# The opening of a fused attention and feed-forward kernel, laid out anew by hand

## The chip, the cores and the metric

The kernel runs on one core of a Trainium2 chip, alone. The metric is the device time of one execution in microseconds; lower is better. The median of three runs before the change is 768.19 us (765.53 to 770.01).

The core's engines are named as in the profile: PE multiplies matrices (PEld loads its weights), DVE and POOL work elementwise, ACT evaluates functions and casts, SP issues DMA transfers. Each works through its own list of instructions in order and waits on semaphores for the others.

## The reference

```python
x = A_x                                             # 2048 x 512
mod = (_silu(c) @ w_mod).reshape(c.shape[0], 6, 1, -1)
sa, ca, ga, sb, cb, gb = (mod[:, 0], ..., mod[:, 5])     # six vectors of 512
h = _layernorm(x, axis=-1) * (1 + ca) + sa
x = x + ga * _A_ref(h, A_wq, A_wk, A_wv, A_wo, A_beta)   # 32 heads of 16, 4 segments of 512 rows, causal softmax plus a memory of earlier segments
h = _layernorm(x, axis=-1) * (1 + cb) + sb
x = x + gb * _B_ref(h, B_w1, B_b1, B_w2, B_b2)           # squared relu, 512 -> 1792 -> 512
```

All is float32. The change concerns what happens before the first attention products: the vectors `ca` and `sa` (numbers 1 and 0 of the six), the normalized first 512 rows, and the weights Wq, Wk, Wv.

## The kernel before

The kernel writes its work as nodes (`op(engine, ...)`), each with an engine, the nodes that it needs and the buffers that it takes. `Plan.run` puts them in order. For each engine a table `ORDER` gives node numbers, and the node at the table's front is taken as soon as its needs are met; behind the table's end the planner goes by priorities. So the table is the order in which an engine's instructions stand in the program, and a node that waits holds up all behind it on its engine.

Numbers are kept exact by splitting: a value is cast to a high part (on ACT), and a subtraction gives the low part (on DVE or POOL); a product is then three matmuls, high by high, high by low and low by high.

The opening, in the order of what needs what:

- The vector c (512 values) is loaded, put through the silu on ACT and DVE, transposed on PE (L532, tile `bcs`) and copied to `cs`, four columns of 128.
- `ca` comes by `mod_cols` and `mod_parts` (L549 to L595): four loads of 256 KB each (`wmod`, L555), one product of four matmuls that fill the four column groups of PE (L570, `bmod`; the "four-fold product" below), a copy on ACT (L574), four matmuls of one column each that sum and turn it (L592), and a DVE instruction that puts it into `modc` (L594). The matmuls are float32 and each appears as two records in the trace.
- `sa` comes by `mod_pieces` (L598 to L614): four loads (L602), and after each of them four matmuls of 128x128 weights by one column (L608). It needs no copy.
- The first 512 rows of x are loaded in four tiles (`xt`, L662), their statistics taken on DVE (L618), the root on POOL (L623), the rows normalized (L627). PE turns them in four groups of four transposes (L640, "turns"). Each turned group is scaled and shifted by `ca` and `sa` (ACT L644 for groups 0 and 2, DVE L647 for 1 and 3), cast to the high part (ACT L650) and given its low part (DVE L651).
- Wq, Wk and Wv are loaded in two transfers each, a first block of 128 columns and the rest (L710). Each has four blocks of columns; ACT casts each (L720), POOL makes the low part (L724; DVE that of Wv's first). The raw Wq lies in `X1L`.
- For the first head group the products of Wq and Wk with all rows are 24 matmuls (L804, two sets of twelve, one for Wq and one for Wk); the later groups take half-height matmuls in groups of six (L810, each pair of sets eight groups), V also in groups of six (L880). Evictions (L841, L843) put the results into `sg`, and transfers on SP ("fills", L859) lay them out in `ST`, whose unused rows six clearing transfers zero beforehand (L736). Score products that find the row maxima (L918, `ba`) follow.
- The two halves of `w1`'s preparation that matter here: a load into `X1L` (L754), which waits until all low parts of Wq are made, and casts and stores of it (L763, L766), piece by piece.

Fillers (L542, `bwarm`) are products of the identity with itself, which nothing reads: 70 of them, placed by the table.

Of the kernel before, what the change touches and what calls it, by code (L numbers as in the profile page):

```python
# [13 lines left out]
ALU = mybir.AluOpType  # L14
# [19 lines left out]
N_WARM = 70  # L34
# [23 lines left out]
8-24 3 25-28 94 29 95-96 30-32 97 33-35 86 36-39 88 117 121 109 113 40-62 283 63-73 284 74-76 285 77 277-280 286  # L58
436-438 322 439 323-324 441 325 442-443 339 353 444 327-330 360 595-596 368 597-598 344 381 600-601 350 602 347 374
603 305-307 356 308 540 371 310-311 465 365 312 386 313 470 721 389 722 377 723 473 393 724 396 860 864 868 479 726  # L60
401 727 476 728 486 497 729 384 405 482 409 406-407 412 500 416 511 419 491 424 513 872 494 624 543 428-430 545 876
552 629 877 548 878 666 879 638 555 432 881 560 882 632 883 503 884 635 645 519 564 669 565-566 521 641 568 1045 575
659 1046 571 1047 578 1048 750 758 535 792 583 1050 764 653 537 587 795 588-589 671 985 1051 678 1052 681 1053 656
909-910 650 911-912 674 755 914-915 686 662 916 761 917 771 779 690-692 767 785 926 694 591 927 943 928 951 929 1120
701 931-932 709 933 1180-1181 957 697 934 1182 776 1183 704 713 988 782 1185 797 1186 800 1187 788 1188 964 978 991
714-715 804 948 1463 1467 954 807 816 812 972 1255 820 817-818 960 827 1315 823 975 1316 830 1317 1078 969 1318 835
1471 1475 1086 1320 1123 1321 1083 981 1322 1099 1113 1323 717 839 994 1126 840 997 1107 841 1001 1089 1004 1092 1009
1013 843 1017 1258 1014 1095 1020 1104 1024 1110 1027 1015 1261 1213 1227 1032 1224 1036-1037 1116 1129 1218 1038 1136
1221 1479 1132 1480 1139 1481 1144 1040 1482 1234 1242 1148-1150 1152 1393 1484 1159 1230 1485 1245 1167 1486 1155
1248 1162 1487 1390 1348 1396 1171-1173 1264 1529-1530 1239 1271 1531-1532 1267 1175 1279 1534-1535 1274 1362 1536  # L70
1251 1537 1356 1512 1369 1513 1377 1514 1591 1515 1359 1353 1283-1285 1287 1517 1290 1294 1518 1380 1519 1365 1520
1374 1648 1383 1649 1546 1650-1651 1297 1302 1554 1653-1655 1386 1560 1656 1551 1306-1308 1783-1784 1399 1310 1402
1785-1786 1567 1575 2070 2074 1788 1406 1588 1409 1789 1557 1790 1414 1791 1578 2066 2078 1418 1563 1581 1594
1419-1420 1572 1681 1723 1422 1918 1429 1919 1432 1920 1686 1425 1921 1695 1437 1923 1692 1441 1597 1924 1600 1925
1584 1926 1689 1702 1442-1443 1707 1604 1607 1716 1726 1616 1713 1612 1617 1620 1858 1698 1618 1729 1623 1710 1627
1630 1445 1816 1639 1635 1821 1732 1640 1861 1824 1735 1641 1739 2082 1742 1830 2083 1747 2084 1719 2085 1837 1851
1643 1751-1752 1864 1753 1755 1845 2087 1758 2088 1827 1762 2089 1765 1993 1770 2090 1848 1833 1774-1776 1842 2111
1951 1959 2112 1867 2113 1854 2114 1965 1874 1778 2116 1882 2117 1877 2118 1870 2119 1956 2240-2241 1962 2187 1972
2242-2243 1980 1968 1886-1888 1986 1890 2245 1983 2246 2145 2247 1996 2248 2150 1893 2128-2129 1897 2130-2131 1977
1900 2133 1905 2134 1989 2156 2135 2166 2136 2180 2177 527 1909-1911 2002 2159 2364 2005 2365 2009 2171 2366 2153 2367  # L80
2012 1913 2369 2017 2370 2174 2371 2162 2372 2290 2301 2021-2023 2025 2311 2032 2488-2489 2295 2028 2490 2183 2491
2040 2304 2035 2493-2494 2298 2269 2044 2277 2495 2190 2496 2193 2045-2046 2197 2274 529 2200 2048 2205 1999 2209 2280
2213 2210-2211 2307 2220 2216 2435 2223 2630 2283 2228 2232-2233 2286 2393 2234 2407 2398 2640 2633-2636 2314 2321
2643-2644 2329 2404 2317 2650 2645-2646 2324 2401 2236 2414 2653 2660 2654-2656 2663 2670 2333-2335 2337 2344 2428
2664-2666 2410 2352 2340 2517 2525 2673-2674 2347 2531 2675 2710 2676 2419 2438 2528 2356-2358 2422 2522 2713 2680
2714-2716 2445 2425 2448 2683-2684 2720 2685-2686 2431 2453 2360 2441 2538 2723 2759 2724 2751 2690 2725-2726 2461
2534 2457 2552 2468 2464 2458-2459 2476 2471 2549 2693 2763 2755 2694-2696 2730 2562 2546 2565 2480-2482 2543 2569
2733-2734 2555 2572 2484 2577 2735 2700 2736 2581 2585 2588 2592 2582-2583 2559 2595 2600 2703-2706 2740 2604-2606
2743 2608 2744-2746 2892 2894 2893 2808 2798 2895 2898 2897 2801-2802 2788 2896 2811 2803 2791 2804 2792 2818 2812
2793 2813-2814 2821-2823 2794 2916 2915 2917 2824 3055 2920 2918 3054 2919 3053 2921 3056 3058 2938 3135 2941 3057  # L90
2939 2943 2940 3059-3060 3123 2942 2944 3065 2961-2962 3063 3061 2967 2963 3071 3069 2964 3070 2965-2966 3067 2985
3073 2984 2987 3075 2986 3131 3072 3077 2990 2989 2988 3074 3078 3127 3081 3007 3076 3009 3008 3082 3012 3079-3080
3010 3013 3084 3011 3030 3088 3032 3031 3083 3036 3086 3085 3090 3033 3035 3092 3089 3087 3094 3163 3091 3095 3093
3034 3165 3098 3096 3166 3099 3167 3100 3103 3164 3104 3102 3097 3107 3190 3108 3168 3106 3115 3169 3112 3388 3101
3184-3185 3105 3186 3109 3188 3187 3189 3311 3380 3118 3205 3208 3206 3313 3310 3207 3392 3211 3317 3210 3209 3312
3226 3314 3316 3227-3228 3384 3230 3324 3229 3329 3322 3231 3318 3247 3232 3315 3248 3320 3250 3326 3249 3328 3333
3327 3252-3253 3331-3332 3337 3251 3330 3271 3335-3336 3268 3273 3270 3269 3341 3334 3340 3272 3339 3289 3292 3338
3345 3290 3274 3344 3343 3349 3291 3295 3342 3346-3347 3353 3293 3348 3294 3350 3421 3420 3649 3352 3424 3422 3357
3351 3641 3356 3354 3361 3423 3637 3355 3359 3358 3363 3426 3365 3425 3375 3360 3441 3364 3372 3442-3443 3445 3444
3362 3366 3369 3447 3446 3463 3467 3568-3569 3464 3462 3466 3567 3468 3570 3465 3571 3574 3483 3486 3485 3484 3573  # L100
3579 3575 3572 3488 3585 3581 3487 3505 3645 3577 3586 3583 3489 3587 3508 3589 3584 3504 3588 3591 3507 3506 3510
3590 3509 3595 3593 3526 3594 3597 3592 3596 3525 3527-3528 3530 3601 3600 3598 3604 3529 3547 3531 3546 3549 3608
3548 3605 3599 3602 3551 3603 3612 3550 3607 3606 3678 3552 3610 3609 3680 3611 3613 3615 3677 3614 3679 3616 3683
# [293 lines left out]
def block_kernel(ctx, tc, x, wq, wk, wv, wo, beta, w1, b1, w2, b2, c, wmod, out):  # L397
# [1238 lines left out]
```

## Time and profile before

| | |
|---|---|
| median of 3 runs | 768.19 us (765.53 to 770.01) |
| profiled execution, its own time | 769.3 us |
| its span, first to last instruction | 767.6 us |
| mean granted PE clock | 0.991 |
| PE busy | 753.6 us, 98% of the span, 6641 instructions |
| DVE, ACT, POOL busy | 585.1, 431.4, 321.5 us |

The profiled execution lies 1.1 us above the median of the runs. The page cuts the span into 40 slices of 19.2 us and prints one digit for each; a nine is 90% or more. Since a waiting matmul's end is modelled, a busy PE need not be a useful one, and fillers count as busy. The timeline gives start and length of each merged group of instructions, and in brackets the idle time of the engine before it and what ended it. The chain of waits goes back from the last instruction to what released it.

### The profile page before, as it was taken

The page shows a single profiled execution, that of the slowest core. Times are in us where ns is not written, and L with a number is a line of the kernel's source. Part 1 is how long each engine was busy: PE and PEld are TensorE (multiplying, and loading weights), DVE is VectorE, ACT ScalarE, POOL GpSimd, SP SyncE. Part 2 cuts the span into 40 slices and gives each one's busy share as a digit, 9 for nine tenths or more (in the row PEclk, how much of TensorE's full clock was granted, in tenths as well). Part 3 has the DMA queues.
Part 4 walks back from the last instruction along what each step waited for, and adds up shares of the span by engine and source line. Part 5 has one row for each costly group of instructions (what it writes and reads, how often), then busy time and mean ns, then how long its engine had stood idle before and what let it go on. Part 6 is the DMA issues. An engine that isn't in the chain of part 4 may idle for free.

```text
span 767.6 us, 17957 instructions
## 1 busy us (share of the span) xinstructions
PE 753.6 (98%) x6641; PEld 607.3 (79%) x6641; DVE 585.1 (76%) x1585; ACT 431.4 (56%) x958; POOL 321.5 (42%) x400
## 2 busy tenths in 40 slices
PE   9999999999999999999999999999999999999997
PEld 7987667765786667776666678998998898989986
DVE  4378898888899887888999986879774875576544
ACT  1558988799978986688856835455211412121110
POOL 4564876688968776366241632351020002000000
PEclk8899999999999999999999999999999999999999
DMA  9478674544665333557573055764552554448721
GB/s 307 160 208 223 202 238 119 156 131 142 173 185 139 96 86 80 172 126 196 173 232 120 3 203 175 287 229 151 192 188 106 188 192 168 151 163 274 273 96 56
DMA packets 61057, 129.65 MB, mean 169 GB/s; under 512 B 8613, under 2 KB 23977, under 8 KB 59178
## 3 DMA queue, kind: packets, MB, share of 16 engines
q1 hardware_dynamic: 60818, 128.37, 52.9%
q8 instruction: 53, 0.87, 0.5%
q14 instruction: 34, 0.28, 0.1%
q10 hardware_dynamic: 152, 0.13, 0.1%
HBM read 81.29 MB, written 20.19 MB: 132 GB/s over the span
## 4 chain that ended last, share of the span: by engine, by line
PE 86%; ACT 4%; DMA 3%; SPq 2%; POOL 2%; DVE 1%; issue 1%; ACTq 0%; POOLq 0%; DVEq 0%
PE bh L1516 18%; PE bqk L810 9%; PE bpv L1146 7%; PE bpf L1579 7%; PE bpf L1578 7%; PE bpf L1580 7%; PE bpb L1087 5%; PE bv L880 5%; PE ba L918 5%; PE bwarm L542 3%; PE bwop L1248 2%; ACT pt L1104 2%; PE bwop L1250 2%; PE bwop L1249 2%; PE bmr L1011 1%
## 5 line engine op out<-in xcount | busy, mean ns | idle before, releaser
L923 DVE CUSTOM_DVE_ANT_0 ba<-ba,msk 128x384 f32<-128x384 f32 (+2 forms) x384 | 192.9, 531 | 35.8 <-PE ba L918 25.1
L1104 ACT ACTIVATE pt<-bpb 128x512 f32<-128x512 f32 x320 | 172.2, 619 | 21.8 <-PE bpb L1087 16.6
L1091 POOL TENSOR_SCALAR_AFFINE_SELECT pt<-pt 128x512 f32<-128x512 f32 x128 | 79.6, 641 | 74.9 <-ACT pt L1104 58.8
L810 PE MATMUL bqk<-HT,WQK 64*128 64x512 f32 x720 | 105.7, 397 | 0.0
L1087 PE MATMUL bpb<-ST 64*128 64x256 f32 (+2 forms) x512 | 79.3, 348 | 2.8 <-DVE sg L843 1.3
L1146 PE MATMUL bpv<-pt,VT 128*32 128x512 f32 (+3 forms) x1024 | 80.3, 437 | 1.1 <-POOL ac L959 0.3
L918 PE MATMUL ba<-ST 63*128 63x256 f32 (+2 forms) x512 | 75.9, 342 | 3.1 <-DMA ST<-sg 1.8
L810 PEld LDWEIGHTS bqk<-HT,WQK 64*128 64x128 f32 x720 | 70.6, 185 | 9.1 <-issue 0.9
L1087 PEld LDWEIGHTS bpb<-ST 64*128 64x128 f32 x512 | 51.3, 186 | 25.1 <-ACT pt L1104 7.4
L1560 ACT CAST ST<-xx 128x512 fp32r<-128x512 f32 x43 | 26.6, 620 | 69.4 <-DVE xx L1552 55.0
L918 PEld LDWEIGHTS ba<-ST 63*128 63x128 f32 x512 | 51.0, 186 | 17.9 <-issue 6.5
L1516 PE MATMUL bh<-ST 128*128 128x256 f32 x420 | 59.1, 282 | 0.0
L1516 PEld LDWEIGHTS bh<-ST,w 128*128 128x128 f32 x420 | 56.2, 190 | 3.4
L1516 PEld LDWEIGHTS bh<-ST 128*128 128x128 f32 x420 | 56.0, 189 | 3.1
L1516 PE MATMUL bh<-ST,w 128*128 128x256 f32 x420 | 58.3, 282 | 0.0
L880 PE MATMUL bv<-WVO,HT 64*128 64x512 f32 x384 | 56.5, 404 | 0.7 <-DVE mx L923 0.7
L1146 PEld LDWEIGHTS bpv<-pt,VT 128*32 128x32 f32 x1024 | 28.7, 109 | 33.6 <-issue 24.6
L923 DVE DVE_READ_ACCUMULATOR2_ANT mx<- 128x1 f32 x384 | 54.2, 141 | 0.0
L1347 POOL TENSOR_TENSOR tt<-h2raw 128x512 f32<-128x512 f32 x8 | 11.0, 1388 | 99.1 <-ACT h2raw L1312 77.7
L1578 PE MATMUL bpf<-w,ST 128*128 128x512 f32 x132 | 52.1, 395 | 0.0
L1579 PE MATMUL bpf<-w,ST 128*128 128x512 f32 x132 | 52.0, 394 | 0.0
L1580 PE MATMUL bpf<-w,ST 128*128 128x512 f32 x132 | 51.7, 391 | 0.0
(210 smaller groups left out, 1630.7 us busy)
## 6 DMA issues: line engine op xcount, KB each, us to landing
ST<-w1d SPq DMA_DIRECT2D x14, 1792.0 KB
w<-w1d SPq DMA_DIRECT2D x14, 1792.0 KB
ST<-sg SPq DMA_DIRECT2D x192, 128.0 KB
w1d<-X1L SPq DMA_DIRECT2D x21, 512.0 KB
xt<-in_A_x SPq DMA_DIRECT2D x16, 256.0 KB
wm<-in_w_mod SPq DMA_DIRECT2D x16, 256.0 KB
xw<-in_A_x SPq DMA_DIRECT2D x16, 256.0 KB
X1L<-in_B_w SPq DMA_DIRECT2D x7, 512.0 KB
```

Source lines behind the costliest of these rows:

```text
L810: nc.tensor.matmul(bank(banks[w]), W3(w, k, x, cols.start, cols.stop)[r], HT[r, y, k], start=first and i == 0, stop=last and i == 2)
L880: nc.tensor.matmul(bank(banks[t]), HT[r, x, k, (t2 + t) * P:(t2 + t + 1) * P], WVO[r, k, y], start=first and i == 0, stop=last and i == 2)
L918: nc.tensor.matmul(dst[:, c0:c0 + n], ST[b:b + 63, 0, sl, qt * P:(qt + 1) * P], ST[b:b + 63, 1, sl, :n], start=True, stop=True)
L923: nc.vector.tensor_tensor_reduce(i, i, msk[:, 512 - n:], scale=1.0, scalar=-3e38, op0=ALU.add, op1=ALU.max, accum_out=o)
L1087: nc.tensor.matmul(dst, ST[b:b + 64, 1, sl, kb * P:(kb + 1) * P], ST[b:b + 64, 0, sl, q0:512], start=True, stop=True)
L1091: nc.gpsimd.affine_select(out=ap, in_=ap, pattern=[[0, ap.shape[1]], [1, P]], compare_op=ALU.is_ge, fill=0.0, base=0, channel_multiplier=-1)
L1104: ns = [op("ACT", 0.49, lambda j=j: nc.scalar.activation(buf("PPP"[n], pt)[:, i + j], bank(keys[j]), AF.Exp, scale=0.25), pr[slot] + 0.01 ...
L1146: nc.tensor.matmul(bank(o)[32 * hq:32 * hq + 32, q0:q0 + src.shape[1]], v[:, a:a + 32], src, start=start, stop=stop, tile_position=(0, 32 ...
L1516: nc.tensor.matmul(pb(i), A[:, x, kk], B[:, y, kk], start=kk == j == 0, stop=kk == 1 and j == 2)
L1578: nc.tensor.matmul(q, rh, wh, start=(i == 0), stop=False)
L1579: nc.tensor.matmul(q, rh, wl, start=False, stop=False)
L1580: nc.tensor.matmul(q, rl, wh, start=False, stop=(i == NF - 1))
```

## The change

Three things change, and nothing behind the opening.

1. `sa` is made as `ca` is, by `mod_cols`; `mod_pieces` is gone.
2. 40 fillers instead of 70.
3. The tables begin with another order. With the numbers shifted for the missing nodes, the lists differ for PE in its first 210 entries of some 1300, for ACT in 130 of 940, for DVE in 87 of 895, for POOL in 53 of 342, for SP in 103 of 403, and are the same behind that. (The trace shows these places before 105 us.)

```diff
-N_WARM = 70
+N_WARM = 40
...
     "PE": """
-8-24 3 25-28 94 29 95-96 30-32 97 33-35 86 36-39 88 117 121 109 113 40-62 283 63-73 284 74-76 285 77 277-280 286
...
+8-30 3 31-33 56 34-37 58 64 82 78 38 66 39-40 90 86 41-47 246-249 252-255 405-408 291 410-413 292-293 308 322 294
...
-    def mod_pieces(m, slot, plus, pr):
-        key, b = ("wmod", m), ("modc", m)
-        loads, n = [], None
-        for k in range(KD):
-            loads.append(sp(lambda k=k: nc.sync.dma_start(buf("P", key)[:, k] if not k else TL[key][:, k],
-                                                          wmod[k * P:(k + 1) * P, m * D:(m + 1) * D]),
-                            pr + 0.001 * k, 1 << 18, get=() if k else [("P", key)], soft=loads[:1]))
-
-        def mm(k):
-            for j in range(KD):
-                nc.tensor.matmul(bank(b)[:, j:j + 1], TL[key][:, k, j * P:(j + 1) * P], cs[:, k:k + 1],
-                                 start=k == j == 0, stop=k == j == KD - 1)
-        for k in range(KD):
-            n = pe("F", 1.05, lambda k=k: mm(k), pr + 0.02 + 0.001 * k, after=[n_cs, loads[k], n], get=() if k else [("#D", b)],
-                   put=[key])
-        return dve(4, lambda: nc.vector.tensor_scalar(modc[:, slot, :], bank(b)[:, 0:KD], plus, None, op0=ALU.add),
-                   pr + 0.05, after=[n], put=[b])
-
...
     n_ca = mod_cols(1, CA, 1.0, PR0 + 0.1, True)
-    n_sa = mod_pieces(0, SA, 0.0, PR0 + 0.2)
+    n_sa = mod_cols(0, SA, 0.0, PR0 + 0.2, True)
```

Lines behind L597 move up by 18: L640 becomes L622, L804 becomes L786, L724 becomes L706, L859 becomes L841.

PE, from the four-fold product of `ca` on, before (xN counts equal matmuls in a row; `bwarm` are fillers, `blnq` turns, `bqk` the first head group's products):

```order
L570 MATMUL bmod<-wmod,cs 32x512 x4
L542 MATMUL bwarm<-ident 128x128 x4
L592 MATMUL bmodc<-selc,t 128x1 x4
L640 MATMUL blnq<-ident,xt 128x128 x16
L542 MATMUL bwarm<-ident 128x128 x23
L804 MATMUL bqk<-HT,WQK 128x512 x3
L542 MATMUL bwarm<-ident 128x128 x11
L804 MATMUL bqk<-HT,WQK 128x512 x3
L542 MATMUL bwarm<-ident 128x128 x3
L804 MATMUL bqk<-HT,WQK 128x512 x3
L542 MATMUL bwarm<-ident 128x128
L804 MATMUL bqk<-HT,WQK 128x512 x15
```

Ahead of these rows stood 17, 4, 1, 3 and 3 fillers, with the transpose L532 and the sixteen matmuls of L608 between them. PE from the same place after the change:

```order
L570 MATMUL bmod<-wmod,cs 32x512 x4
L542 MATMUL bwarm<-ident 128x128 x4
L592 MATMUL bmodc<-selc,t 128x1 x4
L570 MATMUL bmod<-wmod,cs 32x512 x4
L622 MATMUL blnq<-ident,xt 128x128 x8
L542 MATMUL bwarm<-ident 128x128
L592 MATMUL bmodc<-selc,t 128x1 x4
L542 MATMUL bwarm<-ident 128x128 x2
L622 MATMUL blnq<-ident,xt 128x128 x8
L542 MATMUL bwarm<-ident 128x128 x7
L786 MATMUL bqk<-HT,WQK 128x512 x24
L792 MATMUL bqk<-HT,WQK 128x512 x24
```

Ahead of these now stand 23 fillers, the transpose, and three fillers. The 24 products stand in one piece, and those of Wq come before those of Wk (before, nine of Wk's came first). The turns are parted, and the second vector's two steps stand around their first half.

POOL's low parts of the weights, before (raw Wq is `X1L`, raw Wk and Wv are `w`; the second row's order by the table is Wq's block 3, 1, 0, 2):

```order
L624 TENSOR_TENSOR mv<-mv,nhalf 128x2
L724 TENSOR_TENSOR WQK<-w,WQK 128x4x128
L724 TENSOR_TENSOR WQK<-X1L,WQK 128x4x128 x4
L724 TENSOR_TENSOR WQK<-w,WQK 128x4x128
L724 TENSOR_TENSOR WVO<-w,WVO 128x4x128 x3
L724 TENSOR_TENSOR WQK<-w,WQK 128x4x128
```

and after, where the blocks are Wq 0, Wk 0 and 1, Wq 1, Wv 1 to 3, Wq 3, Wk 2, Wq 2:

```order
L606 TENSOR_TENSOR mv<-mv,nhalf 128x2
L706 TENSOR_TENSOR WQK<-X1L,WQK 128x4x128
L706 TENSOR_TENSOR WQK<-w,WQK 128x4x128 x2
L706 TENSOR_TENSOR WQK<-X1L,WQK 128x4x128
L706 TENSOR_TENSOR WVO<-w,WVO 128x4x128 x3
L706 TENSOR_TENSOR WQK<-X1L,WQK 128x4x128
L706 TENSOR_TENSOR WQK<-w,WQK 128x4x128
L706 TENSOR_TENSOR WQK<-X1L,WQK 128x4x128
```

Wq's first block moved from third to first place, Wq's block 2 to the last.

SP's transfers, before (from the seventh on; `ST<-pad` are the clearing transfers):

```order
L555 DMA wmod<-in_w_mod 128x512 x2
L662 DMA xt<-in_A_x 128x512
L555 DMA wmod<-in_w_mod 128x512
L710 DMA w<-in_A_wk 128x4x128
L555 DMA wmod<-in_w_mod 128x512
L710 DMA w<-in_A_wk 128x4x384
L710 DMA w<-in_A_wv 128x4x128
L710 DMA X1L<-in_A_wq 128x4x128
L710 DMA X1L<-in_A_wq 128x4x384
L736 DMA ST<-pad 32x4x512 x4
L710 DMA w<-in_A_wv 128x4x384
L736 DMA ST<-pad 32x4x512 x2
```

and after, from the sixth on (the first seven of `wmod` are the last three loads of `ca` and the four of `sa`):

```order
L555 DMA wmod<-in_w_mod 128x512 x7
L692 DMA X1L<-in_A_wq 128x4x128
L692 DMA w<-in_A_wk 128x4x128
L692 DMA w<-in_A_wk 128x4x384
L692 DMA w<-in_A_wv 128x4x128
L692 DMA X1L<-in_A_wq 128x4x384
L692 DMA w<-in_A_wv 128x4x384
L718 DMA ST<-pad 32x4x512 x2
L535 DMA ge<-in_A_beta 128x32
L718 DMA ST<-pad 32x4x512 x2
L644 DMA xt<-in_A_x 128x512 x2
L841 DMA ST<-sg 32x2x512 x6
```

The loads of `ca` moved ahead of those of `sa`, Wq's first block ahead of the other weights. The third pair of clearing transfers went down among the fills, behind the first store of w1; the w1 load, which stood ahead of the next rows of x and of all fills, now stands behind the first seven fills, and two of the four loads of the next rows of x stand among the fills.

More of the change, by code (lines that the diff above doesn't have):

```diff
@@ L190 @@
+3850
 """,
     "POOL": """
[L192 to L195 removed]
@@ L206 @@
+2320 2312 2319 2718 2413 2420-2421 2510 2425 2444 2443 2448 2436 2735-2737 2537 2738 2545 2544 2549 1970 2560 2568
+2567 2572 2798 2802 3347 2807 2811 2843 3090 2816 2825 2820 2829 2834 2847 2852 2856 3107 3109 2838 3108 3110 3604
+3364 3366 3365 3367 3621-3622 3624 3623
 """,
     "SP": """
[L208 to L209 removed]
```

296 lines of the change are left out of this document (146 added, 150 removed), and 14 rows, old and new, of the table ORDER.

## The prediction

> **What bounds the kernel now.** I read the page's head and slices first, then a table by stretch, then the opening in order of time, then the chain of waits and the DMA issues of SP. Head: busy share of PE, and granted clock by slice.
>
> ```profile
> PE 753.6 (98%) x6641; PEld 607.3 (79%) x6641; DVE 585.1 (76%) x1585; ACT 431.4 (56%) x958; POOL 321.5 (42%) x400
> PEclk8899999999999999999999999999999999999999
> ```
>
> PE is busy for 98% of the span, so only PE time that does nothing, or PE time at a low clock, can be won. The table by stretch says where such time is (columns: stretch, length, busy us and instructions of PE, PEld, DVE, ACT, POOL, granted clock, DMA share, GB/s).
>
> ```profile
> 9.90:13.30 3.40, 3.40 (x33) 3.40 (x32) 1.15 (x3) 0.00 (x0) 0.93 (x2) 1.00 1.07 367
> 14.00:21.00 7.00, 7.00 (x33) 5.11 (x33) 0.66 (x4) 1.10 (x2) 1.26 (x1) 0.50 1.10 344
> 25.00:34.00 9.00, 9.00 (x75) 8.64 (x74) 4.19 (x5) 6.89 (x14) 5.75 (x5) 1.00 0.02 7
> 60.00:70.00 10.00, 9.34 (x87) 7.93 (x83) 8.93 (x30) 7.26 (x23) 2.92 (x5) 1.00 0.76 214
> 70.00:80.00 10.00, 8.44 (x99) 5.97 (x99) 6.90 (x23) 9.19 (x19) 4.94 (x6) 1.00 0.82 229
> ```
>
> The clock is 0.50 from 14 to 21 us, and PE counts as busy throughout the first three rows. What it is busy with, the timeline shows (start, us, engine, line, operation, count):
>
> ```profile
> 1.90 6.22 PE L542 MATMUL bwarm<-ident 128*128 128x128 f32 x34 [1.90 <-POOL ident masks.py:199]
> 10.01 0.47 PE L542 MATMUL bwarm<-ident 128*128 128x128 f32 x2
> 12.02 0.91 PE L542 MATMUL bwarm<-ident 128*128 128x128 f32 x6
> 15.42 1.94 PE L570 MATMUL bmod<-wmod,cs 128*32 128x512 f32 x8
> 17.50 0.58 ACT L574 COPY t<-bmod 128x512 f32<-128x512 f32 x1 [9.03 <-PE bmod L570]
> 19.16 1.71 PE L592 MATMUL bmodc<-selc,t 128*128 128x1 f32 x8
> 20.73 3.30 PE L640 MATMUL blnq<-ident,xt 128*128 128x128 f32 x16
> 20.90 0.16 DVE L594 TENSOR_SCALAR modc<-bmodc 128x4 f32<-128x4 f32 x1 [6.34 <-PE bmodc L592]
> 23.86 5.30 PE L542 MATMUL bwarm<-ident 128*128 128x128 f32 x46
> 29.69 2.62 PE L542 MATMUL bwarm<-ident 128*128 128x128 f32 x22
> ```
>
> L542 is a filler (each is two records). From 23.86 to 32.3 PE runs 34 fillers and three useful products (L804). The useful work proper, which from here on leaves PE almost no pause, begins later, in the chain of waits:
>
> ```profile
> 34.61 3.45 PE bqk L804 x15
> 44.53 1.39 PE bqk L810 x12
> 45.92 0.55 PE ba L918 x8
> 70.90 1.46 PE blnq L640 x12
> 83.01 0.99 PE bmod L570 x8
> 85.23 0.98 PE bmodc L592 x8
> ```
>
> What keeps the useful work back is in POOL and DVE: the low parts of the weights (L724) and of the normalized rows (L651, inputs from L647).
>
> ```profile
> 18.68 1.26 POOL L724 TENSOR_TENSOR WQK<-w,WQK 128x512 fp32r<-128x512 f32 x1 [5.69 <-ACT WQK L720]
> 22.71 0.81 DVE L647 TENSOR_SCALAR lnf<-blnq,modc 128x512 f32<-128x512 f32 x1 [1.65 <-PE blnq L640]
> 26.07 2.50 DVE L651 TENSOR_TENSOR HT<-lnf,HT 128x512 fp32r<-128x512 f32 x4 [1.20 <-ACT HT L650]
> 28.20 5.66 POOL L724 TENSOR_TENSOR WQK<-X1L,WQK 128x512 fp32r<-128x512 f32 x4 [8.26 <-ACT WQK L720]
> 35.07 3.79 POOL L724 TENSOR_TENSOR WVO<-w,WVO 128x512 fp32r<-128x512 f32 x3
> ```
>
> POOL waited 8.26 us for a cast and only then made the four low parts of Wq, to 33.86. The first block of Wq stands third of the four, so the second half of the first head group's products could not start before about 32.5. So the bound of the opening is: modulation vectors at 21.06, low parts of the rows to 28.57, low parts of Wq, while PE fills.
>
> **The change, part by part.** Durations at full clock are from the chain above: a four-fold product 0.99, its four column products 0.98, four turns 1.46/3 = 0.49; a filler record 5.30/46 = 0.115, so a filler 0.23.
>
> *Up to the second vector.* 23 fillers stand first, 46 records: the first 34 took until 8.12, twelve more make 9.50; the transpose of the silu (0.22) and three fillers, 10.41. The first vector's four loads are now fourth to eighth in the queue. Landing: the tenth load of before is the one waited for here.
>
> ```profile
> 10.98 0.69 DVE L618 BATCH_NORM_STATS2 bs<-xt 128x6 f32<-128x512 f32 x1 [1.41 <-DMA xt<-in_A_x]
> ```
>
> At 344 to 367 GB/s (the first two rows by stretch) a load of 256 KB takes some 0.75 us, so the eighth has landed by 9.5 and the twelfth by 12.5. The product of the first vector runs 10.4 to 11.4, its copy (0.14 after it, 0.58) to 12.1 under four fillers (to 12.3), its columns to 13.3; the second vector's product, all loads there, to 14.3; its copy to 15.0 lies under eight turns (to 15.3) and a filler (15.5); columns to 16.5, and the vector (0.16 on DVE) stands at 16.7, against 21.06. The 32 one-column records (L608, two for each product of the order's rows) go, 16 records come. Of the 4.4 us won some 1.7 are clock: at half clock the product and the columns cost 1.94 and 1.71 instead of 0.99 and 0.98 (and the sixteen turns behind them 3.30 instead of 1.96).
>
> Does the clock stay full? In before it halves and returns here (columns: PE busy, clock, DMA):
>
> ```profile
> 13.20:13.40 0.20, 0.20 (x3) 0.20 (x3) 0.20 (x1) 0.00 (x0) 0.00 (x0) 0.70 1.05 369
> 23.40:23.60 0.20, 0.20 (x3) 0.20 (x2) 0.12 (x1) 0.05 (x1) 0.00 (x0) 0.70 1.08 407
> 78.20:81.60 3.40, 2.10 (x30) 1.09 (x28) 2.05 (x6) 2.61 (x7) 0.85 (x2) 1.00 0.21 75
> 296.60:300.00 3.40, 2.53 (x20) 1.44 (x13) 2.65 (x7) 3.24 (x8) 0.00 (x0) 1.00 0.02 5
> 300.00:303.40 3.40, 3.40 (x20) 3.35 (x19) 2.96 (x12) 1.93 (x5) 2.00 (x2) 0.50 0.19 39
> ```
>
> 23.5 less 13.3 is 10.2, and the second dip lasts 3.4, so the clock seems to be judged in steps of 3.4 us. The step to 13.3 held only 4 fillers, 0.9 us; the rest was one-column products. The step to 300 was busy for 2.53 and lost the clock, the one from 78.2 was busy for 2.10 and kept it; since the ends of matmuls are modelled, I count both by records and the spacing of their kind in the chain (0.23 or 0.117) and get about 1.8 for either. So the border lies near 1.8 of 3.4. After the change any 3.4 us between 10 and 17 hold at least 2.25 us of fillers, four-fold products and turns (12.3 to 15.7 is the thinnest): I take the clock as full, and hold half clock as a rival. The Trainium skill, "TensorE: Matmul & The Clock Gate", Part 1: The HAM clock gate, has the clock halve after an idle window of about 3.4 us; by it neither kernel would dip, and this trace disagrees: the row 9.9 to 13.3 shows PE busy for 3.40 of 3.40. The Trainium skill, the same page, Part 4: PE-mode transpose, says that transposes do not count as work for the clock. By that rule the thinnest 3.4 us here would hold 1.25 us, the clock would halve, and the time would be the rival's, 763. The trace speaks against it: the clock returns at 23.5 after a step that held almost only turns.
>
> *Up to the first products.* DVE makes two of the shifted rows (0.81 each, the second after turns that end at 17.4) to 18.4 and the first low part (2.50/4 = 0.63; 0.7 with its start) to 19.1. PE: two fillers, eight turns, seven fillers, 16.5 + 0.46 + 0.98 + 1.61 = 19.5. ACT, at 0.6 a cast and 0.8 a shifted row as in the rows above, has cast the four high parts by about 20.9, so the third low part comes at 21.1 and PE waits 0.3. Wq's and Wk's first low parts are no longer behind anything: their loads are 13th and 14th, casts after 15.0, POOL 15.6 to 18.4 with two of 1.3 to 1.4. All 24 records of L804 then run in one piece: 24 x 0.23 = 5.5, plus waits, to 25.4. Before they ended at 38.06: 12.7 earlier. The 38 fillers among and ahead of them become ten.
>
> *Up to the first score product.* Wk's and Wq's second low parts: casts behind the rows' casts, at 22.2; POOL to 25.0. Then four groups of the second head group (0.70 each) to 28.2; POOL's three parts of Wv (3.79 in all) to 28.9, which costs PE some 0.9; one V group, four and two more groups, 7 x 0.70, to 34.0. That is eleven groups, as many as before had done at 45.92. Gain 12. SP gives the same:
>
> ```profile
> 38.79 5.89 SPq L859 DMA_DIRECT2D ST<-sg  x9
> 16.79 3.81 SPq L736 DMA_DIRECT2D ST<-pad  x2
> 47.37 0.57 SPq L766 DMA_DIRECT2D w1d<-X1L  x1
> 51.14 3.29 SPq L859 DMA_DIRECT2D ST<-sg  x5
> ```
>
> The fills of ST (L859, 0.65 each) wait for the last eviction of the first head group, 25.4 + 0.6 + 0.7: from 26.8 instead of 38.79. The sixth is out at 30.8; before it was out at 42.7, and the score product began 3.2 later, so 34.0 again.
>
> *What is given back.* The third pair of clearing transfers (L736) now stands among the fills: 2.0 us of SP if it goes as the first four did, 3.81 if as this row. Two loads of x, 1.0, stand there too. SP's free time to take that is 47.94 to 51.14, 3.2. Also, PE's pauses between 60 and 80 were 0.66 and 1.56; with everything closer they may grow. I bound the loss between 0 and 4.5 (3.8 + 1.0, almost none hidden) and take 2: SP's slack hides most, and 60 to 80 keeps its pauses. Behind some 105 us the order of all engines is the same, with PE at nearly no pause, so what is left goes to the end: 12 - 2 = 10. The gates' exponential, moved on ACT (0.2), lies beside POOL and costs nothing; without that cover it would cost its 0.2.
>
> The sum stands against one execution of 769.3 (span 767.6): 759.3. The median of the runs is 768.2, 1.1 lower: **758.2**.
>
> **Rivals.**
> *Half clock.* The thinnest 3.4 us fall below the border, be it that turns count for less or that the steps or the loads lie otherwise. If the second vector's product falls to half clock (until 23.5, as before): product to 15.2, turns 16.9, filler 17.4, columns 18.9, vector 19.1, turns to 21.5, seven fillers to 24.2: all is 4.7 later. 768.2 - 12 + 4.7 + 2 = 762.9. For it: the dip is there now; the step's phase is not ours to choose. Against: the thinnest stretch holds 2.25 us.
> *Given back by w1.* The first load of w1 (L754) waits for Wq's last low part, which POOL now makes last: 28.9 + three of 1.37 = 33.0, against 33.86. If that chain set the time at 60 to 80, only 0.9 would stay: 767.3. For it, this store in the chain of waits:
>
> ```profile
> 64.11 4.88 DMA w1d<-X1L
> 41.98 0.62 ACT L763 CAST X1L<-X1L 128x512 fp32r<-128x512 f32 x1
> ```
>
> Against: the load, which cannot have gone out before 33.86, was not used before 41.98, so several us of slack lie there.
> *Slower: the fills land late.* DMA had a share of 0.02 from 25 to 34; now x, fills, clearing and vectors follow without a gap. If each of the first four head groups waits 3 us longer for its fills, 12 are gone: that is the point. The w1 store's 4.88 against at most 3.2 for a fill shows that landing can stretch by 1.7; it would have to be 4 for 768.2 - 12 + 16 = 772.2. Against: share 0.76 and 0.82 at 60 to 80 is not full.
> That it does nothing is ruled out: the fillers are gone from the program.
>
> **How the numbers follow.** Full clock 0.60, half clock 0.25, given back 0.10, slower 0.05. The likeliest's own range is 756.2 (no loss) to 760.7 (4.5 lost); half clock reaches 765.4 with the same loss. Runs shown differ by 4.5, so I go down to 755 and up to 765.4, which leaves out about 2 in 10. Half a per cent, 3.8 us, is about what a measurement of this kernel tells from no change: the border is 764.4. Faster: all of full clock and nearly all of half clock, 0.83; same 0.12; slower 0.05.
>
> **What would show it.** PE with 6641 - 60 - 32 + 16 = 6565 instructions; L804's successor without fillers between, ended by 26; the two vectors by 17; clock 1.00 in slices 1 and 2 but for the first us; POOL's first low part at about 15.6, not 18.7; fills from 27. Wrong would be: clock 0.50 between 13 and 24; the first score product after 38; new pauses of PE between 45 and 70 on DMA or SP that add up to more than 4.

## The result and the profile after

The changed kernel took 756.29 us in the median of 4 runs (755.27 to 757.17) against 766.86 of the kernel before beside it (764.03 to 770.01): ratio 0.986, interval 0.982 to 0.991. The profiled execution took 755.27, its span is 753.5. A second measurement (a1_after_again, six runs) gave 755.36, ratio 0.985 (0.982 to 0.989).

The head of the page of the changed kernel (busy us, share of the span, instructions):

```profile
PE 740.4 (98%) x6565; PEld 594.5 (79%) x6565; DVE 581.2 (77%) x1585; ACT 432.1 (57%) x959; POOL 321.6 (43%) x400
```

The table by stretch of the changed kernel, with the rows that answer to those of before (same columns):

```profile
9.90:13.30 3.40, 3.40 (x30) 2.44 (x29) 1.46 (x3) 0.59 (x1) 0.94 (x2) 1.00 1.11 345
14.00:21.00 7.00, 7.00 (x56) 6.33 (x53) 3.97 (x7) 5.88 (x11) 2.51 (x2) 1.00 1.08 366
25.00:34.00 9.00, 9.00 (x80) 7.13 (x82) 3.95 (x8) 4.76 (x10) 6.81 (x6) 1.00 0.56 138
60.00:70.00 10.00, 9.19 (x89) 6.13 (x88) 9.09 (x27) 7.82 (x18) 7.05 (x10) 1.00 0.74 225
70.00:80.00 10.00, 9.84 (x123) 5.91 (x125) 6.18 (x23) 10.00 (x22) 7.52 (x9) 1.00 0.62 175
```

PE is busy for 98% as before; 13.2 busy microseconds are gone. From 14 to 21 us the clock is 1.00 instead of 0.50, and 56 records run there instead of 33. The timeline of the changed kernel's opening (start, us, engine, line, operation, count):

```profile
1.91 7.62 PE L542 MATMUL bwarm<-ident 128*128 128x128 f32 x46 [1.91 <-POOL ident masks.py:199]
10.47 1.07 PE L570 MATMUL bmod<-wmod,cs 128*32 128x512 f32 x8
15.49 0.95 PE L592 MATMUL bmodc<-selc,t 128*128 128x1 f32 x8
16.48 0.16 DVE L594 TENSOR_SCALAR modc<-bmodc 128x4 f32<-128x4 f32 x1 [2.86 <-PE bmodc L592]
15.73 1.26 POOL L706 TENSOR_TENSOR WQK<-X1L,WQK 128x512 fp32r<-128x512 f32 x1 [4.73 <-ACT WQK L702]
17.70 1.73 PE L542 MATMUL bwarm<-ident 128*128 128x128 f32 x14
19.19 5.73 PE L786 MATMUL bqk<-HT,WQK 128*128 128x512 f32 x24
26.30 3.95 SPq L841 DMA_DIRECT2D ST<-sg  x6
27.72 1.11 PE L862 MATMUL bv<-WVO,HT 64*128 64x512 f32 x6
32.84 0.69 PE L900 MATMUL ba<-ST 63*128 63x256 f32 x8
```

The second vector is there at 16.64 (before 21.06), the 24 records of the first products (L786, before L804) run in one piece to 24.92, POOL starts its low parts at 15.73, the fills at 26.30. The first score product (L900, before L918) starts at 32.84; the timeline of before has it at 45.76 (the row below). That is 12.9 us:

```profile
45.76 0.71 PE L918 MATMUL ba<-ST 63*128 63x256 f32 x8
```

How much of that lasts to the place where the order of all engines is again that of before is told by the first pair of products that spreads a vector (tile `bmodr`), in the view by tile (last figures: the starts of the first and the second of its two records). The kernel before:

```profile
L1401 PE MATMUL bmodr<-t,selc x2: 592/644/696, 112.1 to 112.7; 128*128 128x512 f32 x2
```

The changed kernel, first profiled execution:

```profile
L1383 PE MATMUL bmodr<-t,selc x2: 592/644/696, 103.0 to 103.5; 128*128 128x512 f32 x2
```

The same program in a1_after_again:

```profile
L1383 PE MATMUL bmodr<-t,selc x2: 592/644/696, 100.3 to 100.9; 128*128 128x512 f32 x2
```

Of 12.9 us 9.1 are left in the first execution; in the second, whose first score product came at 32.49 (13.3 earlier), 11.8. What went in between stands in the waits of PE from 30 to 106 us (us in total, times, longest). In a1_after_again:

```profile
PE bpb L1069 <- DMA ST<-mt: 1.4, 1, 1.4
```

In the first execution:

```profile
PE bpb L1069 <- DMA ST<-mt: 1.3, 1, 1.3
PE ba L900 <- DVE sg L825: 0.6, 1, 0.6
```

The table by stretch of the first execution, around these waits:

```profile
47.54:50.95 3.41, 1.45 (x9) 1.10 (x10) 3.04 (x9) 2.25 (x7) 3.21 (x5) 1.00 0.70 194
50.95:54.36 3.41, 3.41 (x23) 3.30 (x22) 1.85 (x3) 2.48 (x5) 2.51 (x4) 0.50 0.80 265
```

PE waits for the transposed maxima (`ST<-mt`) in both. In the first execution it also waits for DVE, is busy for only 1.45 of 3.41 us, and the clock is 0.50 in the 3.41 us behind: another 1.7 us. Its third wait, 0.7 us for ACT, comes near 70 us. Neither execution has the dip that before had at 300 us.

### The profile page after: what moved, and what is told of

It reads as the page before. It is cut to its first block, busy times and chain, and to the rows that moved or that the text cites. A ratio compares the mean times of both kernels' runs of the same rounds, so it can differ in the third digit from the quotient of the medians.

```text
span 753.5 us, 17821 instructions
## 1 busy us (share of the span) xinstructions
PE 740.4 (98%) x6565; PEld 594.5 (79%) x6565; DVE 581.2 (77%) x1585; ACT 432.1 (57%) x959; POOL 321.6 (43%) x400
## 4 chain that ended last, share of the span: by engine, by line
PE 80%; DMA 6%; ACT 5%; POOL 3%; issue 3%; SPq 3%; DVE 0%; ACTq 0%; POOLq 0%; DVEq 0%
PE bh L1498 18%; PE bpv L1128 7%; PE bqk L792 7%; PE bpf L1561 7%; PE bpf L1560 7%; PE bpf L1562 7%; PE bpb L1069 5%; PE ba L900 5%; PE bv L862 4%; PE bwop L1230 2%; ACT pt L1086 2%; PE bwop L1232 2%; PE bwop L1231 2%; DMA ST<-sg 2%; SPq L841 1%
## 5 line engine op out<-in xcount | busy, mean ns | idle before, releaser
L900 PE MATMUL ba<-ST 63*128 63x256 f32 (+2 forms) x512 | 76.0, 341 | 2.7 <-DVE den L1000 0.7
L900 PEld LDWEIGHTS ba<-ST 63*128 63x128 f32 x512 | 51.7, 186 | 17.0 <-ACT pt L1086 2.8
L862 PE MATMUL bv<-WVO,HT 64*128 64x512 f32 x384 | 56.2, 403 | 0.0
```

The source lines that it names most:

```text
L862: nc.tensor.matmul(bank(banks[t]), HT[r, x, k, (t2 + t) * P:(t2 + t + 1) * P], WVO[r, k, y], start=first and i == 0, stop=last and i == 2)
L900: nc.tensor.matmul(dst[:, c0:c0 + n], ST[b:b + 63, 0, sl, qt * P:(qt + 1) * P], ST[b:b + 63, 1, sl, :n], start=True, stop=True)
```

## The experiments

Starts in us of the profiled executions; the medians are of all runs; the ratio is to the kernel before on the same chip. "In" says where the work of `bmodr` starts.

| program | first product | first score product | in | span | median (runs) | ratio, interval |
|---|---|---|---|---|---|---|
| before | 28.92 | 45.76 | 112.1 | 767.6 | 766.1 to 766.9 | 1 |
| e2, fillers cut alone | 24.54 | 44.66 | 112.0 | 766.1 | 763.96 (10) | 0.996, 0.994 to 0.998 |
| f3, order alone | 30.16 | 43.52 | 111.8 | 766.2 | 766.65 (10) | 1.000, 0.998 to 1.001 |
| e3, four-fold products alone | 23.40 | 40.26 | 107.4 | 759.1 | 760.74 (4) | 0.992, 0.989 to 0.995 |
| e1, products and order | 25.29 | 38.63 | 106.4 | 757.0 | 760.12 (4) | 0.991, 0.988 to 0.994 |
| e4, fillers and order | 23.17 | 36.89 | 102.9 | 753.0 | 757.77 (4) | 0.989, 0.985 to 0.993 |
| the change | 19.19 | 32.84 | 103.0 | 753.5 | 756.29 (4) | 0.986, 0.982 to 0.991 |
| a1, the change again | 18.87 | 32.49 | 100.3 | 753.0 | 755.36 (6) | 0.985, 0.982 to 0.989 |
| e5, clearing early | 19.08 | 32.71 | 99.0 | 753.0 | 755.03 (6) | 0.985, 0.981 to 0.988 |
| f4, four fillers less | 18.61 | 32.23 | 99.8 | 749.9 | 754.66 (6) | 0.985, 0.981 to 0.988 |
| e7, both | 18.47 | 32.11 | 99.5 | 750.9 | 752.23 (6) | 0.981, 0.978 to 0.984 |
| a2, both again | 18.91 | 32.54 | 99.0 | 751.3 | 752.77 (6) | 0.980, 0.977 to 0.984 |
| f1, both and w1's cast behind | 18.89 | 32.52 | 99.8 | 751.1 | 753.38 (6) | 0.981, 0.978 to 0.985 |
| f2, both and four more less | 17.96 | 32.06 | 100.7 | 749.8 | 752.72 (6) | 0.982, 0.978 to 0.985 |

What runs behind `bmodr` took 649 to 655.5 us of the span in these executions, with no clear relation to the opening (the three that reach it at 112 took 654 to 655.5, but e5, at 99.0, took 654 too). One profiled execution thus tells the opening, not the end; the profiled execution of e2 was the slowest of its ten, that of f3 too, those of e1, e4 and f4 the fastest of theirs.

### The thirty fillers put back

```diff
 PE:  eight turns, 7 fillers,
+     30 fillers,
      first product of the first head group (L786)
```

> The changed kernel with 70 fillers again: the 30 extra ones stand together ahead of the first head group's 24 products. Theory A (the opening is a chain: vectors, low parts of the rows, products, and what reaches the first score product later reaches the end later, less what pauses behind it swallow): 30 x 0.23 = 6.9 us stand in the way of the first product (19.2 becomes 26), about 0.5 of it is taken back where PE waits for Wv's low parts, so the first score product comes at about 39 instead of 32.8, and the end is 4.5 to 6.5 later than the changed kernel: about 761 to 763. Theory B (the opening's lead is mostly swallowed by waits before 100 us, so the end hardly sees it): less than 2 us later, 756 to 758. Theory C (the whole gain is the clock): no change, 756.

PE in e1, from its timeline:

```profile
17.11 8.43 PE L549 MATMUL bwarm<-ident 128*128 128x128 f32 x74
38.63 0.74 PE L907 MATMUL ba<-ST 63*128 63x256 f32 x8
```

74 records, 60 of them put back, and the first score product 5.8 us later than in the changed kernel (6.4, if the first 46 filler records, 0.6 us faster in this execution, had taken as long). Measured 760.12, 3.8 us more than the change in its first measurement and 4.8 more than in its second: just below A's 761, and well above B's 758. So fillers are PE time that passes to the end, less 2 to 3 us; PE had no wait ahead of the first score product with them and none without.

### The fillers cut alone

```diff
-N_WARM = 70
+N_WARM = 40
 PE (order of before):  ... sixteen turns,
-     23 fillers, three products, 11 fillers, three products, 3 fillers, three products, 1 filler, fifteen products
+     8 fillers, 24 products
```

> The kernel before with 40 fillers: of the 38 behind the turns 8 stay, all ahead of the first product; nothing else changed. Theory A: Wq's first low part is ready only at 32.5, so the second set of products starts at about 32.6 instead of 34.6, with PE pausing some 3 us ahead of it; the end 0.5 to 2 us earlier than before, or nothing if the pause costs a step at half clock (1.7): 765 to 767. Theory D (the fillers are the cost: 30 x 0.23): 6 to 7 us earlier, about 760.

PE in e2, from its timeline:

```profile
24.54 0.50 PE L810 MATMUL bqk<-HT,WQK 128*128 128x512 f32 x1 [0.60 <-ACT HT L656]
31.11 5.83 PE L810 MATMUL bqk<-HT,WQK 128*128 128x512 f32 x13 [3.27 <-POOL WQK L730]
44.66 1.04 PE L924 MATMUL ba<-ST 63*128 63x256 f32 x8
```

The table by stretch of e2:

```profile
26.47:29.88 3.41, 1.38 (x6) 0.77 (x5) 2.24 (x2) 3.41 (x9) 3.18 (x3) 1.00 0.00 0
29.88:33.29 3.41, 2.18 (x5) 1.79 (x6) 0.00 (x0) 0.45 (x1) 3.41 (x3) 0.50 0.00 0
```

The same 6.9 us of fillers are gone, but now PE waits 0.60 us for a cast of the rows and 3.27 for a low part of Wq on POOL, and from 29.88, within that pause, the clock is 0.50 again, for two steps. The first score product comes 1.1 us earlier, not 6.9. Over ten runs, of which this execution was the slowest, 2.9 us are won, between A's 765 to 767 and D's 760: under the old order the fillers covered a wait.

### The order alone

```diff
 PE (order of the change):
-     four-fold product of sa ... its columns
+     sixteen one-column products of sa (32 records)
      ... eight turns, 7 fillers,
+     30 fillers,
      first product of the first head group
```

> The order of the change with 70 fillers (the 30 ahead of the first product of the first head group, all in one piece) and with the one-column products for the first vector: the order by itself, the corner that the other runs leave out. Fillers alone gave 2.9 us, products alone 6.2, fillers and order 9.1, products and order 6.8. If the three shares added up, the order alone would be worth 10.6 - 2.9 - 6.2 = 1.5 us, 765. Theory P (the order only pays once the fillers are gone, since PE would else come to the products late enough for the old order): within 1 us of before, 766 to 767.5. If order is what carries the gain: below 763.

PE in f3, from its timeline:

```profile
12.67 4.36 PE L615 MATMUL bmodc<-cs,wmod 128*128 128x1 f32 x32
16.88 1.95 PE L647 MATMUL blnq<-ident,xt 128*128 128x128 f32 x8
21.61 8.79 PE L549 MATMUL bwarm<-ident 128*128 128x128 f32 x74
43.52 0.73 PE L925 MATMUL ba<-ST 63*128 63x256 f32 x8
```

The waits of PE in f3 from 30 to 106 us:

```profile
PE bpb L1094 <- DMA ST<-mt: 1.8, 1, 1.8
PE ba L925 <- DMA ST<-sg: 1.7, 1, 1.7
```

766.65 against 766.48 beside it: theory P, nothing. The order brings the weights' first low parts earlier, but PE still has its list of fillers and one-column products to run, at half clock in the turns (eight in 1.95, in the changed kernel in 1.09); the 2.2 us that it had at the first score product it waited away behind it. With the fillers cut the same order is worth 6.2 us (e2 763.96, e4 757.77).

### The four-fold products alone

```diff
-n_sa = mod_pieces(0, SA, 0.0, PR0 + 0.2)
+n_sa = mod_cols(0, SA, 0.0, PR0 + 0.2, True)
 PE (order of before): the product stands where the fourth piece stood, its columns ahead of the product of ca
```

> The kernel before with the second vector by a four-fold product: the product stands where the last of the sixteen one-column matmuls stood, its columns ahead of the first vector's product; 70 fillers, weights and loads ordered as before. Theory A: the step to 13.3 us now holds work, the clock stays full, vectors at about 16.5 instead of 21.1, POOL's low parts of Wq from 23 instead of 28.2, all about 5 earlier; first score product at about 41 instead of 45.9; end 4 to 5 earlier, about 762. If the clock halves all the same: within 1 of before. Theory C (the whole gain is the clock): 9 to 11 earlier, about 756.

PE in e3, from its timeline:

```profile
13.62 1.20 PE L577 MATMUL bmod<-wmod,cs 128*32 128x512 f32 x8
40.26 0.71 PE L907 MATMUL ba<-ST 63*128 63x256 f32 x8
```

A four-fold product at 13.62 takes 1.20 where before took 1.94, and the first score product comes 5.5 us earlier. The half-clock stretch from 13.3 to 23.5 is gone (it had cost 5.1), as are some 1.5 us of one-column work (3.6 us of it, less 2.0 for the product and columns in its place); against that, the first 34 records of fillers took 6.83 instead of 6.22. Measured 760.74: 6.2 us less, nearest to A's 762. The mean granted clock was 1.0 or 0.999 in all four runs; in the 13 runs of before beside it 0.990 to 0.998.

### The one-column products put back

```diff
-n_sa = mod_cols(0, SA, 0.0, PR0 + 0.2, True)
+n_sa = mod_pieces(0, SA, 0.0, PR0 + 0.2)
 PE (order of the change):
-     four-fold product of sa, four turns, ..., its columns
+     sixteen one-column products of sa, four turns, ...
```

> The changed kernel with the second vector by sixteen one-column matmuls again, all at the place of the four-fold product. Theory A: PE has 3.7 us of one-column matmuls behind 1 us of columns, so one step of 3.4 us holds almost no work and the clock halves at about 17; the turns and fillers behind it cost double until about 20 to 23; first product at 23 to 25 instead of 19.2, first score product at 36 to 38, end 3 to 5 later than the changed kernel: 759 to 761. Theory D (only the number of fillers counts): no change, 756. If the clock stays full: 1.5 to 2 later.

PE in e4, from its timeline:

```profile
14.01 3.71 PE L614 MATMUL bmodc<-cs,wmod 128*128 128x1 f32 x32
19.87 1.91 PE L646 MATMUL blnq<-ident,xt 128*128 128x128 f32 x8
36.89 0.82 PE L924 MATMUL ba<-ST 63*128 63x256 f32 x8 [0.17 <-DMA ST<-sg]
```

The row by stretch of e4 in which the clock is at half:

```profile
18.38:21.79 3.41, 3.41 (x18) 3.41 (x17) 1.50 (x3) 1.92 (x3) 0.00 (x0) 0.50 1.07 377
```

The stretch of one-column work brings back one step of half clock, 1.7 us; the prediction's rival, half clock in the opening, had counted 4.7. The first score product comes 4.0 us later than in the changed kernel, of which the first group of fillers, slower in this execution, makes 0.73; yet `bmodr` is level with the first execution of the change, and 2.6 behind the second. The median of e4 is 1.5 to 2.4 us above the change's, between D's 756 and A's 759 to 761, but its four runs reach from 754.7 to 760.7, and the change was not run beside them. So it is not shown how much of the 4 us that these products win in the opening arrives once fillers and order are in place; without the cut of the fillers they are worth 6.2 (e3) and 6.5 (e1 against f3).

### The change again, and the third clearing pair moved

```diff
 SP:  two loads of x,
+     third clearing pair (ST<-pad),
      first six fills, ... load of w1, ... 
-     third clearing pair (ST<-pad),
      two transfers of maxima (ST<-mt)
```

> The changed kernel itself, beside the next two, so that they are compared on one chip: 755 to 757.5, about 10 below the kernel before.

> The changed kernel with the third pair of clearing transfers moved from among the fills (43.6 us) to behind the first two loads of the next rows of x, where SP has nothing to do from 20.4 to 26.3. Theory A (what is given back behind 33 us is SP and the DMA queue: the maxima's rows go out at 45.0 behind this pair and land 4.9 us later, PE waits 1.3 and then loses a step of clock, 1.7): the rows go out at 43.7 and land in 3 to 4, the dip at 50 to 55 goes, end 1 to 3 earlier than the changed kernel. Rival E (DVE's and ACT's work sets 40 to 50, SP is only the messenger): within 0.5.

PE's wait for the maxima in e5, from the waits of PE from 30 to 106 us:

```profile
PE bpb L1075 <- DMA ST<-mt: 0.2, 1, 0.2
```

The wait fell from 1.4 to 0.2 us, and `bmodr` started 1.3 us earlier; this is the give-back that the prediction put on this pair. Of the six profiled executions with the pair among the fills (the change, a1, e1, e4, f3, f4) five wait 1.2 to 1.8 us there, all but e4; of the five with the pair moved (e5, e7, a2, f1, f2) none waits more than 0.2. But the time is 755.03 against 755.36, inside the spread of either (753.2 to 756.4, 754.7 to 756.5): by the time the rival E, that nothing reaches the end, is the nearer one, though the wait that theory A named was there and went.

### Fewer fillers

```diff
-N_WARM = 40
+N_WARM = 36        # e7 and a2, with the clearing pair moved; f4, without; f2 has 32
 PE:
-     23 fillers, transpose of the silu
+     19 fillers, transpose of the silu
```

> As the one with the early clearing, and four of the 23 fillers in front less. Theory A: the first vector's loads have landed by 9.5, so product, vectors and first products all come 0.9 earlier (first product at 18.3 instead of 19.2); end 0.5 to 0.9 earlier than with the early clearing alone. If the loads are not there, or the step of the clock now holds too little: no change or up to 5 later.

> The same program as e7_clear_early_four_less, as the reference for the runs beside it. It gave 752.2 us, 14.5 less than before. Every theory expects 751.5 to 753.0 here; 754.5 or more would say that the step from 755.0 to 752.2 was chance (its profiled run had the first score product only 0.6 us earlier than e5_clear_early).

> The changed kernel with 19 front fillers instead of 23 and the third clearing pair left where the change put it. If the 2.8 us between e5_clear_early and e7_clear_early_four_less come from the fillers alone, 752.3 to 753.5. If the pair matters too (theory G: 2 us of SP among the fills), 754 to 755, 1.5 to 2.5 more than with the pair moved.

> e7_clear_early_four_less with 15 front fillers instead of 19. Theory F (front fillers are on the path as long as the loads are ahead of them): the first four-fold product starts about 0.8 us earlier, at 9.0, and 0.5 to 0.9 us go. Rival D (the eighth load lands at about 8.7 to 9.5 by the bytes moved in the profile): PE waits for the load, and less than 0.3 us goes; a second half-clock step from the pause would add up to 1.7.

The four-fold product of `ca` in a2, from its timeline:

```profile
10.19 1.06 PE L576 MATMUL bmod<-wmod,cs 128*32 128x512 f32 x8
```

The same product in the timeline of f2, with a wait of its weight load:

```profile
8.47 1.84 PE L575 MATMUL bmod<-wmod,cs 128*32 128x512 f32 x8
9.26 0.14 PEld L575 LDWEIGHTS bmod<-wmod,cs 128*32 128x32 f32 x2 [0.54 <-DMA wmod<-in_w_mod]
```

Both together beat the change: the 12 runs of e7 and a2 lie between 749.7 and 753.8, the 10 runs of the change between 754.7 and 757.2. Four fillers are 0.9 us; the rest of the 3 us is not in the opening, where the first score product came at 32.11 and 32.54, against 32.49 and 32.84 in the change; at `bmodr` they are 0.8 and 1.3 ahead of a1. The clock does not explain it: the mean granted clock over the runs was 0.9993 and 0.998 in e7 and a2, 0.996 and 0.998 in the two measurements of the change. A thousandth is 0.75 us, so it could be some 1 of the 3 us between e7 and a1, but nearly nothing between a2 and a1. Without the moved pair (f4) the median is 754.66, the value that theory G named, but its runs reach from 751.6 to 759.3, so how the gain divides between pair and fillers stays open. With 15 fillers (f2) the product starts at 8.47 but takes 1.84 instead of 1.06, since its last loads have not landed (0.54 of idle on PEld); most of its lead over e7 is gone again at the first score product (32.06 against 32.11), and the time is the same: D, the loads are next.

### w1's cast put behind the casts of the gates

```diff
 ACT: two evictions of maxima (mt),
-     second cast of w1,
      two casts into sg,
+     second cast of w1,
```

> e7_clear_early_four_less with one instruction moved on ACT: the second cast of w1 (256 columns, waiting 2.63 us for a store of w1 to land, until 46.28) goes behind the two casts of the second pass's gates that stood behind it. Theory W (the transfers of w1 hold ACT, ACT holds DVE's difference, and PE waits 1.40 us for it at 49.03): that wait goes, 0.7 to 1.5 us less than the program with the cast in front. Rival L (the landing of the transposed maxima, on SP behind the fills, is next): the wait changes its name and the time stays within 0.5.

In the changed kernel the load and the store of w1 do hold ACT, ACT holds DVE, and DVE holds PE. Its timeline (the bracket: idle before, and what ended it):

```profile
31.84 0.39 SPq L736 DMA_DIRECT2D X1L<-in_B_w  x1
37.98 0.62 ACT L745 CAST X1L<-X1L 128x512 fp32r<-128x512 f32 x1 [2.41 <-DMA X1L<-in_B_w]
45.45 0.41 ACT L745 CAST X1L<-X1L 128x256 fp32r<-128x256 f32 x1 [1.85 <-DMA w1d<-X1L]
46.87 1.29 DVE L825 TENSOR_TENSOR sg<-bqk,sg 128x512 fp32r<-128x512 f32 x2 [1.33 <-ACT sg L823]
48.21 0.50 PE L900 MATMUL ba<-ST 63*128 63x512 f32 x1 [0.65 <-DVE sg L825]
```

In e7 PE's wait for DVE was longer, by the waits of PE from 30 to 106 us:

```profile
PE ba L906 <- DVE sg L831: 1.4, 1, 1.4
```

In f1 another of nearly that size stands in its place, for a copy on ACT:

```profile
PE bpb L1075 <- ACT pk L1027: 1.1, 1, 1.1
```

753.38 against 752.77: nothing won, much as L expected of the time, though the wait that came was not the one that L named. And in a2, the same program as e7, PE waited for neither: ACT stood 0.96 us for the store of w1 there, 2.63 in e7. The wait depends on when the transfers of w1 land in an execution; it is not what separates these kernels.

## Why the prediction was right, point by point

Predicted 758.2 (755.0 to 765.4); measured 756.29 and 755.36. The likeliest case came, full clock. The opening went as worked out; that the total came so close is partly luck, as the last points show.

*Up to the second vector.* 16.7 predicted, 16.64 measured; the stations ahead of it, too (fillers to 9.50 and 9.53, product of `ca` from 10.4 and 10.47, columns from 15.5 and 15.49). The clock was 1.00 in the thinnest stretch. The Trainium skill's rule that transposes do not count ("TensorE: Matmul & The Clock Gate", Part 4: PE-mode transpose) would, with the border of 1.8, have had it at half; the clock stayed full. This tests the rule only weakly: counted back in steps of 3.413 from the half clock at 50.95, one step ran from 13.40 to 16.82, and without its turns it held about 1.7 us, close to that border. The stronger row is the prediction's own, of the clock that returns behind turns. e4 shows what the rival could cost: with one-column work in that place one step of half clock came back.

*Up to the first products.* 19.5 to 25.4 predicted, 19.19 to 24.92 measured. The wait of 0.3 for the third low part did not come: the 24 records ran without a gap.

*Up to the first score product.* 34.0 predicted, 32.84 measured. From the products' end to there I had 8.6 us, eleven groups and 0.9 for POOL's parts of Wv; it took 7.9. The term that was too large is the wait for Wv: POOL made its parts at 24.26 to 28.06, ahead of the last parts of Wq and Wk, and PE lost about 0.25 (1.11 us for six records of L862 instead of 0.87). So 12.9 us were won instead of 12.

*What is given back.* Taken as 2, bounds 0 and 4.5. Against the 66.3 us of before from the first score product to `bmodr`, the changed kernel took 67.8 (a1) and 70.2: 1.5 and 3.9, of which 1.7 is a step of half clock at 51 us. The step that I had not seen is that one: I asked for the clock in the opening only, and not whether a pause of PE behind it, which I had allowed for, would be paid twice. The clearing pair was named rightly as a cause of a wait (e5), but its 1.3 us did not show in the time. So the 2 was a middle between bounds, and the two executions lie on either side of it.

*The sum.* 759.3 for the profiled execution of before, lowered by 1.1 to the median. The changed kernel's medians lie 1.9 and 2.8 below 758.2. Of this, 1.3 to 1.5 is that before itself measured 766.9 and 766.7 beside the change, not 768.2; against these the gain is 10.6 and 11.4, where 10 was forecast. The sum's last step, that what is left at 105 us goes to the end, did not hold for the profiled pair: 9.1 at `bmodr`, 14.1 at the end. By the starts of the score products 4.5 of these 5.0 us arise between 290 and 330 us. There the profiled execution of before waited for a fill (waits of PE from 270 to 330 us) and lost the step of half clock at 300:

```profile
PE ba L918 <- DMA ST<-sg: 1.8, 1, 1.8
```

It is not the change that mends this: e2, with the order of before, gains 3.8 us in the same stretch. So that execution of before was a slow one there.

*The rivals.* Given back by w1: its chain is in the trace and costs 0 to 1.4 us from one execution to the next, not 9. Fills that land late: PE's longest waits from 30 to 106 us, down to 0.2, hold none for a fill in the two executions of the changed kernel.

*What carried the gain.* I argued part by part as if the parts added; the runs with one or two of the three changes show that they do not. Fillers alone 2.9, order alone 0, the two together 9.1; products alone 6.2, with the order 6.8, all three 10.6 to 11.4. Fillers and products without the order were not run; in e3 POOL makes Wq's four low parts from 23.00 to 28.68, so the third, for which e2 waited, is there at about 27.3. With the fillers cut the first head group could then end some 1.9 us before e3's 32.5 (an estimate: 27.3, 0.2 to the start as in e2, and thirteen products at the 5.73 / 24 = 0.24 of the changed kernel), not 6.9.

PE never waits from 1.9 us to the first score product in before or after, so the opening is the sum of PE's records: 60 filler records at 0.115, 6.9; 10.2 us at half clock, 5.1; some 1.5 of one-column work; 13.5 in all against 12.9 measured. The order adds nothing to that sum; it lets the fillers go without a wait in their place.

The half clock weighs less over the runs than in this pair of traces. In e2, whose PE runs as before does until the turns are done, it lasted two steps in the opening (12.82 to 19.65), not three, and the changed kernel gives some back behind the opening. The mean granted clock was 0.995 in the 48 runs of before beside the experiments, 0.996 and 0.998 in the change: 3.8 us lost against 3.0 and 1.8. So by this estimate the clock is 1 to 2 us of the gain, fillers 6.9 and one-column work 1.5, in all 9.2 to 10.4 of the 10.6 to 11.4; what makes up the last microsecond stays open.

## What to carry to other kernels

Where an engine does not pause, its time is the sum of its instructions, and bringing their inputs earlier wins nothing; where it runs fillers, ask of each what wait it covers and move that input first, then cut (here 2.9 us without, 9.1 with). As in the opening of before, a stretch of thin matrix work can halve the clock though the engine counts as busy, and a pause of two microseconds can be paid again as a step of half clock behind it. Judge a few microseconds by the medians of several runs and place them by the trace: two profiled executions of the same program stood 2.7 us apart at 100 us.

## What the runs showed of the hardware

In these traces half clock comes in steps of 3.41 us, one, two (6.83) or three (10.24) in a row. It came behind stretches in which PE was busy for 1.45 (the changed kernel) or 1.38 of 3.41 us (e2), and, by the table by stretch of f2, behind one in which it was busy for 2.97 with 81 short records:

```profile
88.06:91.47 3.41, 2.97 (x81) 2.10 (x67) 3.23 (x15) 3.41 (x9) 2.78 (x3) 1.00 0.71 177
91.47:94.88 3.41, 3.41 (x20) 3.05 (x22) 2.38 (x5) 2.53 (x6) 2.51 (x2) 0.50 0.74 226
```

So no single border of busy time fits: the prediction's row from 78.2 us was busy for 2.10 and kept the clock, this one for 2.97 and lost it. Eight of the 81 records are one-column products, as ahead of the dip in before. Whether the prediction's border of 1.8, which it counted by records and not by busy time, holds here is not shown. The Trainium skill, "TensorE: Matmul & The Clock Gate", Part 1: The HAM clock gate, asks for an idle window of about 3.4 us; none of these stretches was idle for that long, so the measurement decides against it here.

The first fillers run at about half the speed: their records start 0.213 us apart, later ones 0.112. For how long differs by execution: the same 46 records, which wait for nothing once the identity is there, took 7.03 us in e1 and 8.35 in e4. The timeline of e1:

```profile
1.90 7.03 PE L549 MATMUL bwarm<-ident 128*128 128x128 f32 x46 [1.90 <-POOL ident masks.py:199]
```

The timeline of e4:

```profile
1.91 8.35 PE L548 MATMUL bwarm<-ident 128*128 128x128 f32 x46 [1.91 <-POOL ident masks.py:199]
```

The same page, same part, says that the window runs freely, so that the moment of full clock depends on where the first product falls in it, and gives 500 ns to either side of about 4 us. Here the spread is larger: the records' spacing changes at 5.3 us in e1 and at 8.1 in e4, which is 3.4 and 6.2 us behind the first filler. Counting back in steps of 3.413 us from the half clock at 56.54 in e1 and at 18.38 in e4 gives the same two moments (5.34 and 8.14). All that follows on PE is shifted by the 1.3 us between the two groups.
